# Crossbar turns of q', k' and x for pairs 5 to 11 in a gated recurrence followed by a GELU layer, with the whole order of the work written out

## The chip, the cores and the metric

The kernel runs on one core of one Trainium2 chip. The metric is the device time of one execution in microseconds; before the change the median of three runs is 177.12 us (177.09 to 177.12). Profiles and traces come from one further execution, recorded by the hardware profiler; its times start at the first instruction.

## What is computed

```
# q, k, v, alpha: (4, 8, 768, 48) f32; w_in: (384, 2048); w_out: (2048, 384)
for t in range(768):
    state = alpha[:, :, t, :, None] * state + k[:, :, t] (x) v[:, :, t]     # outer product, 48 x 48 a head
    y[:, :, t] = q[:, :, t] @ state
x = y with the 8 heads of a token side by side                              # (3072, 384)
out = gelu_tanh(x @ w_in) @ w_out                                           # (3072, 384) f32
```

Four sequences, eight heads of 48 features, 768 time steps; each head carries a 48 by 48 state that decays by alpha per feature. The result feeds two dense layers.

## The kernel before

**Chunks and pairs.** Time is cut into 6 chunks of 128 tokens. A *pair* is one chunk of two sequences; there are 12, m = 0 to 11, pair m being chunk m // 2 of sequences 2(m % 2) and the next. A *unit* is one sequence of a pair. Within a chunk the recurrence becomes matrix products:

- `ln` (ScalarE, L361): the logarithm of alpha; `cum` (TensorE, L378): its running sum over the tokens, by a product with a triangle of ones. In all but the last chunk `cum` also makes, with L380, the sums over the whole chunk, feature by feature, in eight products of one column a pair.
- `b`, `binv` (ScalarE, L407): the exponentials of plus and minus the running sum, in bf16; `bend` (L401): that of the whole chunk's sum, which `end` (VectorE, L516) spreads into the two halves of 64 features.
- `qp`, `kp` (VectorE, L418): q' = q b and k' = k binv, each head padded to 64 features.
- the turn of q' and k' so that features lie on partitions. For pairs 0 to 6 TensorE does it: `t` (L428) are transposes into PSUM, `ev` (L446) the eviction into `qkT`. For pairs 7 to 11 (`TURN_QK`) the crossbar does it: `turn` m.0 (q') and m.1 (k'), transposing DMAs issued by the SP queue (L466).
- `attn` (TensorE, L489): 16 products on half arrays of 64 rows, giving the scores of both units; `mask` (VectorE, L496) keeps the causal half.
- `y` (TensorE): four products of 96 columns with the carried state (L543) and eight of 48 columns with v (L546) for each unit; `x` copies the result into bf16 (L553).
- the turn of x: for pairs 0 to 5 on TensorE (`tx`, L560, and `xe`, L564), for pairs 6 to 11 (`TURN_X`) by one DMA for each unit (L472).
- `kv` (TensorE, L506) and `st` (VectorE, L528 and L531): the state for the next chunk.
- `l1` (TensorE, L572): first dense layer of the pair, 8 tasks of 6 products; `gelu` (ScalarE, L578) after each; `l2` (TensorE, L591): second layer, 4 tasks of 4 products a unit; `ot` (copy out of PSUM, L603) and `store` (SP queue, L616). Pairs 0 and 1 share one second layer, named `l20`.

A task is named by kind, pair and number: `attn5.0` is the score task of pair 5, `l15.0` the first task of its first layer, `store2.0` a store of pair 2's first unit.

**Loads.** 66 loads. The first 12 are issued by SP and ScalarE; the rest by POOL, in the order of `LOADS`, with two gates near the start only (`gatea 0 1`, `gatek 0 1`): a small POOL copy that waits for an early load, so that later ones do not overtake it. A load of a, q, k or v of a pair takes 384 KB from HBM; v is narrowed to bf16 on the way. Each kind has five or six buffers (`BUFS`), and a load waits until its buffer's last reader is done.

**Order.** `Scheduler.order` decides the order in which every engine gets its tasks, on paper, before the program is built. Up to some 46 us the order is written out by hand in `FIRST` ("P:attn0.0" is TensorE, V VectorE, A ScalarE, G POOL, S the SP queue). After that a list scheduler takes over with the costs in `W` and `COST`; `late_qk` and `late_x` are allowances by which it takes a crossbar turn of an early pair to land later. Each engine then works off its own list strictly in order, and waits where an operand or a buffer isn't ready. The SP queue issues turns and stores in one list. `DECAYS` groups the logarithms and exponentials of pairs between two runs of gelus, since ScalarE must load a table whenever it changes between them.

Of the kernel before, what the change touches and what calls it, by code (L numbers as in the profile page):

```python
# [16 lines left out]
    cum=530, cum_packed=1500, t8=450, t4=225, attn=340, kv=170, inter=170, intra=205, tx=168, l1_4=655, l1_2=340, l2=655,  # L17
    qk2=910, qk1=500, ev8=650, ev4=350, mask=640, st=1090, st0=545, end=110, attn2=590, vb=320, vb_act=480, ring=1300, ring_issue=670, out=2050, lead=600, receipt=1400, receipt_hw=1000, xc=520, xe=330, ot=540,
    ev8_act=960, ev4_act=520, xc_act=450, xe_act=450, ot_act=450,
    strip=1700, cast=1900, weight=2080, dma=2100, issue=1100, wissue=760, sp=100, store=2600, turn=1250, landed=2200, xbar_qk=1500, xbar_x=1000, late_x=2500, late_qk=1200, piece=330, late_k=1500, piece_issue=450, begin=620, cast_0=1300, share=1200, cast_1=1900, ln_packed=1040, cold=380, fill=216, zero=1100,  # L20
# [26 lines left out]
class Scheduler:  # L47
# [16 lines left out]
    def order(self):  # L64
# [5 lines left out]
        def given(tag):  # L70

            n, at = len(taken[tag]) - self.bufs[tag], 0
            for u in taken[tag][n] if n >= 0 else ():
                if u.done is None:
                    return None
                at = max(at, u.done)
            return at

        def ready(t, inorder=True):
# [7 lines left out]
            for tag, _ in t.takes:  # L87
                g = given(tag)
                if g is None:
                    return None  # L90
                at = max(at, g)
# [80 lines left out]
class _Kernel:  # L172

    BLOCKS = ((0,), (1,), (2,), (3,), (4,), (5,), (6,), (7,), (8,), (9,), (10,), (11,))
    DECAYS = {-1: (0, 1), 1: (2, 3), 2: (4,), 3: (5,), 4: (6, 7), 5: (8,), 6: (9,), 7: (10,), 8: (11,)}

# [10 lines left out]
        A:table.0 A:load.2 A:load.3 S:load.0 S:load.1 S:load.4 A:ln0.0 S:load.5 P:fill.7 P:cum0.0 A:ln0.1 G:gate.0 G:load.12 S:load.6 P:cum0.1 A:b0.0 S:load.7  # L187
        A:bend0.0 V:qp0.0 A:binv0.0 A:binv0.1 S:load.8 V:kp0.0 P:fill.2 P:t0.0 A:b0.1 V:ev0.0 P:fill.1 P:t0.1 S:load.9 A:ev0.1 V:qp0.1 S:load.10 A:bend0.1
        P:fill.3 P:attn0.0 V:kp0.1 G:gate.1 S:load.11 P:t0.2 G:load.13 V:mask0.0 A:ev0.2 P:t0.3 G:load.14 V:mask0.1 A:ev0.3 P:fill.1 P:t0.4 V:ev0.4 P:fill.1
        P:attn0.1 A:ln1.0 G:load.15 P:t0.5 V:mask0.3 P:cum1.0 A:ev0.5 G:load.16 V:vb0.0 A:ln1.1 V:end0.0 P:y0.0 V:mask0.2 G:load.17 P:kv0.0 A:binv1.0 P:cum1.1  # L190
        V:st0.0 A:x0.0 G:load.18 A:vb0.1 V:kp1.0 P:tx0.0 A:b1.0 P:y0.1 V:xe0.0 G:load.19 V:qp1.0 P:t1.1 A:x0.1 A:bend1.0 G:load.20 A:b1.1 P:fill.1 P:t1.0
        A:ev1.0 V:ev1.1 G:load.21 V:qp1.1 P:fill.1 P:kv0.1 V:st0.1 G:load.22 A:binv1.1 P:tx0.1 P:attn1.0 V:xe0.1 G:load.23 P:t1.2 V:kp1.1 P:l10.0 A:ev1.2
        G:load.24 V:mask1.0 P:t1.3 A:bend1.1 P:t1.4 V:mask1.1 G:load.25 A:ev1.3 P:l10.1 V:ev1.4 G:load.26 A:vb1.0 P:t1.5 P:attn1.1 G:load.27 V:ev1.5 P:y1.0
        G:load.28 P:l10.3 V:end1.0 V:vb1.1 V:mask1.2 G:load.29 A:gelu0.0 P:kv1.0 P:l10.2 V:mask1.3 A:x1.0 G:load.30 P:l10.5 A:gelu0.1 V:st1.0 A:gelu0.3 P:y1.1
        G:load.31 P:l10.4 A:gelu0.5 V:x1.1 P:tx1.0 A:gelu0.2 P:tx1.1 P:l10.6 G:load.32 V:xe1.1 A:gelu0.4 V:xe1.0 P:l10.7 A:gelu0.6 G:load.33 P:l11.0 A:gelu0.7
        P:l11.6 A:gelu1.0 P:l11.5 A:gelu1.6 P:l11.7 A:gelu1.5 P:l11.2 A:gelu1.7 P:l11.4 A:gelu1.2 P:l11.3 A:gelu1.4 P:l11.1 A:gelu1.3 P:kv1.1 P:l20.0
        A:gelu1.1 P:l20.4 P:l20.1 A:ln2.0 P:l20.2 P:cum2.0 P:l20.5 A:b2.0 A:binv2.0 P:l20.9 A:bend2.0 V:kp2.0 A:ln2.1 P:l20.6 V:st1.1 P:cum2.1 V:qp2.0 P:l20.8
        A:b2.1 A:binv2.1 P:t2.0 P:l20.3 V:kp2.1 A:ev2.0 V:qp2.1 P:l20.10 A:bend2.1 P:attn2.0 P:t2.1 V:mask2.1 P:l20.7 A:ev2.1 V:mask2.0 P:l20.14 A:ln3.0
        P:attn2.1 P:y2.0 V:mask2.2 P:l20.13 V:mask2.3 P:l20.12 V:x2.0 P:cum3.0 A:ot0.0 V:ot0.1 P:y2.1 A:ot0.2 S:store0.0 S:store0.1 P:tx2.0 P:l20.11 A:x2.1
        S:store0.2 V:xe2.0 A:b3.0 P:tx2.1 P:l20.15 V:xe2.1 A:binv3.0 V:end2.0 P:l12.0 V:ot0.3 A:bend3.0 P:l12.1 V:qp3.0 S:store0.3 P:kv2.0 P:l12.2 V:st2.0  # L200
        A:gelu2.0 P:l12.3 V:end3.0 V:kp3.0 A:gelu2.1 P:l12.4 A:gelu2.2 P:t3.0 A:gelu2.3 P:t3.1 A:gelu2.4 V:ev3.0 P:l12.5
# [9 lines left out]
    TURN_QK, TURN_X = (7, 8, 9, 10, 11), (6, 7, 8, 9, 10, 11)  # L211
# [10 lines left out]
    BUFS = dict(ca=1, yk=2, ff=4, la=3, qp=4, kp=4, b8=2, kn=2, qkT=4, atm=6, x=3, ot=5, bend=3, ends=8,  # L222
                a=6, q=5, k=5, vb=6)

    def __init__(self, ctx, tc, q, k, v, alpha, w_in, w_out, out):
# [22 lines left out]
        self.ones = const.tile([C, 1], F16, name="ones")  # L248
# [3 lines left out]
        self.half = const.tile([C, 2], F32, name="half")  # L252
        self.state = [[const.tile([C, H // 2, 2 * D], BF16, name=f"st{b}_{i}") for i in range(2)]
                      for b in range(B)]
        self.ring = {n: [const.tile([C, 2, H, 64], F16 if n == "la" else BF16, name=f"{n}{i}")
                         for i in range(self.BUFS[n])] for n in ("la", "qp", "kp")}
# [54 lines left out]
    def wait(self, r, m, j):  # L311

        u = self.p[list(self.p)[m]]
        return lambda e: self.nc.gpsimd.tensor_copy(self.gate[:, 0:1], u[r][:, j, 0, 0:1])
# [606 lines left out]
```

## Time and profile before

| | |
|---|---|
| median of three runs | 177.12 us |
| span of the profiled execution, first to last instruction | 175.3 us |
| what lies around the span, against the median | 1.8 us |
| first product of l10.0, TensorE | 16.91 us |
| last product of the second layer ends, TensorE | 172.66 us |
| POOL's last load issued | 88.28 us |
| first crossbar turn issued (x of pair 6) | 93.11 us |
| median from issue to landing: turn of q' or k' | 2.8 us |
| median from issue to landing: turn of x, one unit | 2.3 us |
| median from issue to landing: loads of a, q, k, v by POOL | 11.6 to 12.5 us |
| TensorE clock granted | 1.00 throughout |

How to read the profile: the page gives each engine's busy time, then the span in 40 equal slices (4.4 us each) whose digits are tenths busy, then DMA queues, then the chain of work that ended last. q0 is the queue of POOL's loads, q1 that of the transfers issued by SP; a DMA's packets are spread over 16 DMA engines, and shares of a short stretch can exceed 100% because packets of the two queues overlap on an engine. A product's duration includes its way through the array, so a run of products is priced by the distance between starts. "PE" is TensorE, "PEld" its weight loads, "DVE" VectorE, "ACT" ScalarE, "POOL" GpSimd, "SPq" the SP queue.

### The profile page before, as it was taken

The numbers are of one execution on the slowest core, as the hardware profiler recorded it, in microseconds if no ns is written. First come the engines' busy times: TensorE is split into PE (matmuls) and PEld (weight loads), VectorE is DVE, ScalarE is ACT, GpSimd is POOL, SyncE is SP. The second block draws the span as 40 slices with busy tenths as digits, with TensorE's granted clock in tenths as the row PEclk, the third lists the DMA queues.
The fourth block names the chain that finished last, engine by engine and source line by source line (L and its number), as shares of the span: only waits on it lengthen the run. The fifth ranks groups of instructions, "written<-read, shape, count | busy, mean of one in ns | idle before, by whom it ended". The sixth has DMA issues, their size and how long they took to land.

```text
span 175.3 us, 4440 instructions
## 1 busy us (share of the span) xinstructions
PE 170.4 (97%) x1845; PEld 135.4 (77%) x1845; DVE 96.8 (55%) x192; ACT 128.9 (74%) x213; POOL 57.7 (33%) x64
## 2 busy tenths in 40 slices
PE   7989999999999999999999999999999999999993
PEld 2667999667987896797798698698697697796973
DVE  6499920356888993795598897495426405000000
ACT  4677999666968668768788967977987984481941
POOL 2496348977645776576720000000000000000000
PEclk9999999999999999999999999999999999999999
DMA  4999999999999999999999992271271360401102
GB/s 138 307 262 224 210 243 238 246 205 207 249 273 204 242 256 220 217 226 199 200 264 224 200 136 80 54 172 52 47 187 28 90 165 4 115 20 49 45 0 90
DMA packets 49620, 28.86 MB, mean 165 GB/s; under 512 B 37696, under 2 KB 46016, under 8 KB 49600
## 3 DMA queue, kind: packets, MB, share of 16 engines
q0 software_dynamic: 26464, 17.70, 60.8%
q1 hardware_dynamic: 22592, 10.49, 24.8%
q10 hardware_dynamic: 544, 0.39, 0.8%
q8 instruction: 14, 0.23, 0.6%
q14 instruction: 6, 0.05, 0.1%
HBM read 25.17 MB, written 4.72 MB: 170 GB/s over the span
## 4 chain that ended last, share of the span: by engine, by line
PE 90%; DMA 6%; DVE 1%; issue 0%; ACT 0%; SPq 0%; POOL 0%
PE hT L572 36%; PE acc L591 36%; DMA v<-in_v_dram 4%; PE at L489 4%; PE qkT_ps L428 3%; PE yps L546 3%; PE kv L506 2%; PE yps L543 2%; DMA a<-in_alpha_dram 2%; PE cum L378 2%; PE xT_ps L560 1%; PE cum L380 1%; SPq L305 0%; ACT qkT L446 0%; DVE vb L389 0%
## 5 line engine op out<-in xcount | busy, mean ns | idle before, releaser
L572 PE MATMUL hT<-xT,w_in 128*128 128x256 bf16 x576 | 69.4, 273 | 0.0
L578 ACT ACTIVATE gT<-hT 128x512 bf16<-128x512 f32 x96 | 56.3, 600 | 17.7 <-PE hT L572 14.2
L591 PE MATMUL acc<-w_out,gT 128*128 128x384 bf16 (+3 forms) x416 | 69.0, 313 | 0.0
L572 PEld LDWEIGHTS <-w_in 128*128 128x128 bf16 x576 | 61.1, 114 | 1.6
L591 PEld LDWEIGHTS <-gT 128*128 128x128 bf16 x416 | 36.9, 98 | 19.2
L496 DVE TENSOR_TENSOR atm<-at,ut 128x512 bf16<-128x512 f32 x48 | 30.1, 681 | 12.7 <-PE at L489 12.6
L418 DVE TENSOR_TENSOR qp<-q,b 128x768 bf16<-128x768 f32 (+1 forms) x15 | 11.9, 794 | 14.0 <-ACT b L407 11.7
L418 DVE TENSOR_TENSOR kp<-k,binv 128x768 bf16<-128x768 f32 (+1 forms) x15 | 11.9, 791 | 10.6 <-ACT binv L407 10.6
L603 ACT COPY ot<-acc 128x384 f32<-128x384 f32 (+3 forms) x17 | 7.4, 439 | 13.0 <-PE acc L591 12.9
L308 POOL DMA_DIRECT2D k<-in_k_dram x11 | 12.2, 1107 | 6.6 <-DVE atm L496 3.0
L308 POOL DMA_DIRECT2D vb<-in_v_dram x11 | 12.1, 1102 | 6.7 <-PE hT L572 1.7
L308 POOL DMA_DIRECT2D q<-in_q_dram x11 | 12.2, 1109 | 6.1 <-DVE atm L496 1.3
L308 POOL DMA_DIRECT2D a<-in_alpha_dram x11 | 12.2, 1114 | 5.9 <-DMA w_in<-in_moe_w_in_dram 1.3
L407 ACT ACTIVATE b<-cum 128x768 bf16<-128x768 f32 (+1 forms) x15 | 10.3, 683 | 3.6 <-PE cum L380 2.3
L280 ACT ACT_TABLE_LOAD x9 | 11.5, 1283 | 0.9 <-PEq L905 0.7
L578 ACT ACT_TABLE_LOAD x9 | 11.5, 1283 | 0.2
L407 ACT ACTIVATE binv<-cum 128x768 bf16<-128x768 f32 (+1 forms) x15 | 10.2, 681 | 0.1
L528 DVE TENSOR_TENSOR stmp<-kv,st 128x384 f32<-128x384 f32 x16 | 8.8, 552 | 2.0 <-PE kv L506 2.0
L553 DVE CAST x<-yps 128x384 bf16<-128x384 f32 x12 | 6.7, 556 | 4.7 <-PE yps L546 4.7
L531 DVE TENSOR_TENSOR st<-stmp,ends 128x384 bf16<-128x384 f32 x16 | 8.9, 558 | 0.6
L446 ACT COPY qkT<-qkT_ps 128x512 bf16<-128x512 bf16 (+1 forms) x9 | 6.5, 728 | 3.7 <-PE qkT_ps L428 3.5
L546 PE MATMUL yps<-vb,atm 128*128 128x48 bf16 x192 | 8.7, 183 | 0.4 <-DVE vb L389 0.4
(65 smaller groups left out, 156.7 us busy)
## 6 DMA issues: line engine op xcount, KB each, us to landing
out_dram<-ot SPq DMA_DIRECT2D x19, 192.0 KB, 5.2
a<-in_alpha_dram POOLq DMA_DIRECT2D x9, 384.0 KB, 12.5
q<-in_q_dram POOLq DMA_DIRECT2D x9, 384.0 KB, 11.6
k<-in_k_dram POOLq DMA_DIRECT2D x9, 384.0 KB, 11.7
vb<-in_v_dram POOLq DMA_DIRECT2D x9, 192.0 KB, 11.6
w_in<-in_moe_w_in_dram POOLq DMA_DIRECT2D x4, 384.0 KB, 9.3
w_out<-in_moe_w_out_dram POOLq DMA_DIRECT2D x4, 384.0 KB, 11.1
out_dram<-ot SPq DMA_DIRECT2D x9, 96.0 KB, 1.8
```

What stands on the lines that cost most here:

```text
L280: nc.scalar.add_instruction(mybir.InstLoadActFuncSet(name=nc.get_next_instruction_name(), act_func_set_id=i, engine=mybir.EngineType.Activ ...
L308: dma(u[t][:, lo:hi].rearrange("t b h d -> t (b h) d"), src.rearrange("b h s d -> s (b h) d")[c * C:(c + 1) * C])
L407: self.nc.scalar.activation(u[n].rearrange("t i h d -> t i (h d)")[:, lo:hi], cum, AF.Exp, scale=1.0 if n == "b" else -1.0)
L418: self.nc.vector.tensor_tensor(out, rows, b, op=ALU.mult)
L496: self.nc.vector.tensor_tensor(u["atm", i][:, o], u["at", i][o], self.ut[:, None, :].to_broadcast([self.C, self.H // 2, self.C]), op=ALU.mult)
L528: nc.vector.tensor_tensor(s, acc, old, op=ALU.add)
L531: nc.vector.tensor_tensor(new.rearrange("f p (o d) -> f (p o) d", o=2), acc.rearrange("f p (o d) -> f (p o) d", o=2), ends, op=ALU.mult)
L546: nc.tensor.matmul(y[:, h, :], u["atm", i][:, h % 2, h // 2, :], u["vb"][:, i, h, :], start=c == 0, stop=True, skip_group_check=True)
L572: self.nc.tensor.matmul(h[:, s], w_in[:, j, nt % 4 + s], self.xT[c % self.NX][:, j, lo:hi].rearrange("p g t -> p (g t)"), start=j == 0, st ...
L578: return lambda e: self.nc.scalar.activation(self.gT[c % self.NG][:, nt:nt + 2, lo * self.C:hi * self.C], f.pop(("h", c, lo, nt)), AF.Gelu ...
L591: self.nc.tensor.matmul(f["acc", c, b][:, lo:hi], self.gT[c % self.NG][:, nt, b * self.C:(b + 1) * self.C], self.w_out[:, nt, lo:hi], star ...
L603: self.copy(e)(f["ot", c, b][:, sl], f["acc", c, b] if half is None else f["acc", c, b, half][:, sl])
```

## The change

- The crossbar turns q' and k' of pairs 5 to 11 (before 7 to 11) and x of pairs 5 to 11 (before 6 to 11), and x as one DMA for both units of a pair; the layout of `xT` becomes unit by unit.
- The chunk's end decay is no longer a product and an exponential: from pair 2 on, four small VectorE transposes (`tr`) of 32 by 32 blocks take the last row of `b`, which is now kept in f32 in a padded ring; `end` reads from that. L380 and, from pair 2 on, `bend` are gone.
- For pairs 3 to 11 (`INTER`) the product with the carried state becomes part of the task `attn`: 16 products of 64 rows and 48 columns into two PSUM tiles, one for each half of the heads; `y` adds the eight products of its half of the heads for both units.
- `FIRST` now holds the whole order to the end, tasks of the two layers of neighbouring pairs interleaved; `DECAYS` is gone.
- `LOADS` is unchanged; all loads are issued in the order of their numbers. `wait` and `held` learn to wait for a turned tile, and no entry of `LOADS` uses that.
- The last pair's second unit is now done before its first; the program ends with `ot11.0` and `store11.0`, a whole 128 by 384 tile.

```diff
@@ the order, the part around the first two crossbar pairs (A ScalarE, P TensorE, V VectorE, S the SP queue)
+        P:cum4.0 A:b4.0 A:binv4.0 V:mask3.1 P:y3.0 P:l22.5 P:l22.6 V:x3.0 V:qp4.0 P:y3.1 A:x3.1 P:l22.3 P:cum5.0 V:kp4.0 P:tx3.1 P:tx3.0 V:xe3.1
+        A:ot2.0 P:l22.7 V:xe3.0 P:t4.1 V:tr4.0 A:binv5.0 V:kp5.0 P:t4.0 P:l13.0 A:b5.0 V:ev4.1 S:store0.0 V:tr4.1 V:tr4.2 V:tr4.3 V:ev4.0 V:end4.0
+        A:ot2.1 S:turn5.1 S:store2.0 P:l13.7 A:gelu3.0 A:gelu3.7 P:kv4.1 P:l13.2 P:l13.5 P:l13.6 P:kv4.0 A:gelu3.2 S:store0.1 V:st4.1 A:gelu3.6
+        A:gelu3.5 P:l13.1 P:l13.4 A:gelu3.1 P:l13.3 A:gelu3.4 V:st4.0 V:qp5.0 V:tr5.0 P:attn4.0 V:mask4.2 S:turn5.0 V:mask4.0 V:mask4.1 V:mask4.3
+        P:l23.4 A:gelu3.3 P:l23.5 P:l23.6 P:y4.0 P:l23.7 V:tr5.1 V:ot3.1 V:tr5.2 A:ln6.0 P:y4.1 P:cum6.0 P:l23.0 A:x4.0 V:tr5.3 V:end5.0 A:x4.1
+        P:tx4.1 V:xe4.1 S:store3.1 S:store0.3 A:binv6.0 P:tx4.0 V:xe4.0 P:l23.1 V:kp6.0 P:kv5.0 P:l23.2 A:b6.0 A:ln7.0 V:st5.0 P:l14.0 P:kv5.1 P:l23.3
+        P:l14.7 A:gelu4.0 A:ot3.0 A:gelu4.7 P:l14.1 A:gelu4.1 V:st5.1 G:load.47 G:load.48 G:load.49 P:attn5.0 G:load.50 G:load.51 V:tr6.0 S:turn6.1
+        S:store2.1 P:l14.6 P:l14.4 V:qp6.0 V:mask5.0 V:mask5.1 S:turn6.0 A:gelu4.6 P:l14.3 P:l14.5 A:gelu4.4 A:gelu4.3 A:gelu4.5 P:l14.2 V:tr6.1
+        V:mask5.2 V:mask5.3 P:y5.0 P:y5.1 P:l24.4 V:x5.0 V:x5.1 V:tr6.2 P:cum7.0 P:kv6.1 A:gelu4.2 P:l24.0 P:l24.1 P:kv6.0 V:tr6.3 V:end6.0 V:st6.1
+        A:b7.0 P:l24.5 P:l24.6 V:qp7.0 A:binv7.0 V:st6.0 A:ln8.0 P:cum8.0 A:b8.0 A:binv8.0 P:l24.7 P:l24.2 P:l24.3 P:attn6.0 A:ot4.1 S:turn5.2 V:tr7.0
...
+        P:l211.6 P:l211.7 P:l211.8 P:l211.9 V:ot10.0 S:store10.0 P:l211.0 S:store10.1 V:ot11.1 A:ot11.2 V:ot11.3 S:store11.1 S:store11.2 S:store11.3
+        P:l211.1 P:l211.2 P:l211.3 A:ot11.0 S:store11.0
...
-    TURN_QK, TURN_X = (7, 8, 9, 10, 11), (6, 7, 8, 9, 10, 11)
+    TURN_QK, TURN_X = (5, 6, 7, 8, 9, 10, 11), (5, 6, 7, 8, 9, 10, 11)
+    INTER = (3, 4, 5, 6, 7, 8, 9, 10, 11)
...
-        self.xT = [const.tile([C, self.NKT, B, C], BF16, name=f"xT{c}") for c in range(self.NX)]
+        self.xT = [const.tile([C, B, self.NKT, C], BF16, name=f"xT{c}") for c in range(self.NX)]
...
-                for p in range(H // 2) if u["sums"] else ():
-                    nc.tensor.matmul(cum[:, i, H * D + p:H * D + p + 1],
-                                     la[:, i, 2 * p:2 * p + 2, :].rearrange("t h d -> t (h d)"),
-                                     self.ones, start=True, stop=True, skip_group_check=True)
...
-    def turn_x_dma(self, u, i, c, b):
-        return lambda e: self.nc.sync.dma_start_transpose(self.xT[c % self.NX][:, :, b, :], u["x", i])
+    def turn_x_dma(self, u, c, b):
+        return lambda e: self.nc.sync.dma_start_transpose(
+            self.xT[c % self.NX][:, b:b + 2].rearrange("d u j t -> d (u j) t"), u["x"].rearrange("t u n -> t (u n)"))
...
+            if carried:
+                c, b = carried
+                y = [self.tile("yk", [C, 2, H // 2, self.D], F32, "yps") for _ in range(2)]
+                for i in units:
+                    st = self.state[b + i][c % 2]
+                    for p in range(H // 2):
+                        for o in range(2):
+                            sl = slice(64 * o, 64 * o + 64)
+                            nc.tensor.matmul(y[o][:, i, p, :], u["T"][sl, 0, i, p, :], st[sl, p, self.D * o:self.D * o + self.D],
+                                             start=(i, p) == (0, 0), stop=False, skip_group_check=True)
...
+    def last_row(self, u, o, half):
+        C, H, D = self.C, self.H, self.D
+        def emit(e):
+            if "tr" not in u:
+                u["tr"] = self.tile("kn", [C, H, 64], F32, "tr")
+            rows = u["rows"][96:128]
+            lo, f = o * D + 32 * half, 64 * o + 32 * half
+            self.nc.vector.transpose(u["tr"][f:f + 32, :, 0:32], rows[:, lo:lo + H * 2 * D].rearrange("t (g n) -> t g n", n=2 * D)[:, :, 0:32])
+        return emit
...
+    def y_heads(self, u, o):
+        def emit(e):
+            y = u["y", o]
+            for i in range(2):
+                for p in range(self.H // 2):
+                    self.nc.tensor.matmul(y[:, i, p, :], u["atm", i][:, o, p, :], u["vb"][:, i, 2 * p + o, :],
+                                          start=False, stop=True, skip_group_check=True)
+        return emit
...
-        s = self.s = Scheduler(self.BUFS, self.fill, 60000, self.FIRST, self.LANDED)
+        s = self.s = Scheduler(self.BUFS, self.fill, 0, self.FIRST, self.LANDED)
```

## The prediction

> **What bounds the kernel now.** I read the page's busy shares first, then the 40 slices, the waits of TensorE, the chain, and last the DMA view by stretches.
>
> ```profile
> span 175.3 us, 4440 instructions
> ...
> PE 170.4 (97%) x1845; PEld 135.4 (77%) x1845; DVE 96.8 (55%) x192; ACT 128.9 (74%) x213; POOL 57.7 (33%) x64
> ...
> PE   7989999999999999999999999999999999999993
> ...
> DMA  4999999999999999999999992271271360401102
> ...
> PE 90%; DMA 6%; DVE 1%; issue 0%; ACT 0%; SPq 0%; POOL 0%
> ```
>
> TensorE is busy in every slice from the fourth to the last but one, the chain is TensorE for 90%, and asked for TensorE's waits between 20 us and the end, the trace names none. From 17 us on the time is the sum of TensorE's instructions, and what keeps that so is that every operand lies ready before its product's turn comes. The second long row of nines is the DMA's: full until the 24th slice, about 100 us, because the 66 loads run without a break (the last is issued at 88.28 us and lands some 11 us later). Until 93 us this kernel puts no transpose on the DMA engines. The change does.
>
> A few rows tell what a transfer of the SP queue meets there. First the stretch 94 to 95 us, loads still running, with one turn of x started at 93.11 (packets, MB, share; then us to landing):
>
> ```profile
> q0 software_dynamic: 302, 0.19, 115.9%
> q1 hardware_dynamic: 82, 0.02, 10.7%
> ...
> xT<-x SPq DMA_TRANSPOSE x1, 5.9
> ```
>
> Then 99 to 100 us, loads over, turns alone:
>
> ```profile
> q1 hardware_dynamic: 1173, 0.28, 128.4%
> ```
>
> q0 carries POOL's loads, q1 what SP issues. In a microsecond beside loads q1 gets 82 packets through, alone 1173: a fourteenth. Over 94.2 to 96 us it is 133 packets, 8.3 for each of 16 engines in 1.8 us, **0.22 us a packet and engine**; alone it is 0.014. Stores of 192 KB (144 packets, 9 an engine) say the same of the time between 40 and 90 us: 143 packets of q1 in 62 to 65.5 us are 0.39 us each, 288 in 73 to 78 us are 0.28; they land after 5.2 to 8.9 us, against 1.9 once the loads are over. I take 0.3, with 0.22 and 0.39 as ends.
>
> **What the change takes from TensorE.** All prices are distances between starts in the timeline.
> - The column sums (L380): four products from 69.34 to the next start at 69.45, 27 ns each, 8 a pair, 8 pairs: 64 x 0.027 = 1.7 us gone.
> - q' and k' of pairs 5 and 6: 16 transposes from 59.01 to the next start at 59.90, 0.89 us a pair: 1.8 us gone. x of pair 5: two times 0.17, 0.34 us gone.
> - The product with the carried state, pairs 3 to 11: before, two times four products of 96 columns, 0.17 us each, 0.34 a pair. After, 16 products on half arrays, 48 columns each. No row shows it. Ends: one weight load after another at L380's 27 ns, 16 x 0.027 = 0.43; or two halves side by side, as the sixteen half-array products of L489 need 0.555 against the eight's 0.33, that is 0.028 each for 128 columns, so by columns 0.17. I take 0.22, nearest to L489, which is the same form on the same tile: 0.12 x 9 = 1.1 us gone (ends: 1.5 gone, 0.8 added).
>
> [...] No run here has the 48-column form yet.
>
> Sum: 4.9 us less. TensorE's last product ends at 172.66 us now and would end at 167.8.
>
> **What is moved off the path and costs nothing there.** Four small transposes a pair on VectorE (bounds: 0.16 us as the 16-element row of L516, 0.55 as a 384-element f32 row; I take 0.3, 32 of them 9.6 us) against 2.8 us of evictions of pairs 5 and 6 and 0.7 of pair 5's x: 6 us more on an engine that is 55% busy; at 0.55 a pair costs 2.2 us, still within VectorE's idle time (28 of 62 us between 92 and 154). ScalarE loses the bend exponentials and two of 18 table loads (1.28 us each). The f32 decays enter products that already read one f32 operand. x as one turn of six blocks instead of two turns of three saves an issue of 1.2 us on SP. All of it is hidden by a TensorE that waits for none of it; should VectorE fall behind, masks come late, which belongs to the rivals.
>
> **Tail.** The last unit now ends with one 384-column copy (0.476 against 0.212) and one 192 KB store (1.9 against 1.5): 0.7 us more after the last product, 3.3 instead of 2.6.
>
> **What is added: a wait.** That no load waits for a turn changes nothing by itself: the list of loads and its two gates are the same in both kernels, and the new code that could hold a load for a turn is not used. TensorE takes its list in order, and attn5.0 now waits for the crossbar. Summing the new list with the prices above from l10.0 at 16.9 us, and shifting by the 0.8 us that such a sum lacks against the trace by then, attn5.0's turn comes at **74 us**. On SP stand, in order, store0.0, turn5.1 (k'), store2.0, store0.1, turn5.0 (q'). kp5.0 is ready at 58.3, qp5.0 at 64.3 by the same sum. A turn of q' or k' is eight blocks: between 139 and 143.8 us two of them account for 2176 small packets, so 1088 each, 68 an engine. From 58.3: issue 1.3, the store ahead 2.7, k' 68 x 0.3 = 20, two stores 5.4, q' 20 again: 108 us. That lies past the end of the loads, and there the price falls to 0.014. So the end of the loads decides. They drain at about 97 us now (in 96 to 99 us q0 has only 17% left); the new order issues them back to back and no buffer holds them (all but the last v, which needs y5, find their buffers free before attn5.0), and the turns' own packets add some 150 x 0.02 = 3 us an engine. Loads over at about 100; q' lands at 99 to 101.5. With 0.22 us a packet it lands at 96. I take 99.5: **TensorE stands for 25.5 us** at attn5.0. Behind it wait l14.6 and everything after, on ScalarE the gelus, on VectorE mask5; POOL doesn't wait. k', q' of pair 6 and x of pair 5 queue behind, but by then the queue is quick and attn6.0 is 11 us further on: no second stall of size.
>
> [...]
>
> After so long an idle time TensorE may start slow: the first seven idle products of the program take 3.26 us, where 512 columns at the later pace (256 in 0.109) would make 1.53. I add 1.6 us, between nothing and 1.7.
>
> Sum against the profiled execution: 167.8 + 25.5 + 1.6 + 3.3 = 198.2 us of span. The median of the runs, 177.12, is 1.8 above the span of 175.3, so **200.0 us**. With q' landing between 92 and 104, and the product of pairs 3 to 11 at its ends: 191 to 207.
>
> **Rivals.**
> - *The turns keep up* (faster). Place: attn5.0. It decides at the pace: 154 packets an engine (k', two stores, q') in the 14.4 us from 59.6 to 74 allow 0.094 us a packet. If transposed packets go through at that or better, no stall is left beyond some tenths, and the time is 177.1 - 4.9 + 0.7 + 0.3 = 173.2. For it: turns alone need 0.014, and the planner's own allowance is only 1.2 us more for pairs under 8. Against: every stretch with loads shows over twice 0.094. Chance 0.15.
> - *Half a stall*: loads with many 96-byte packets (v) let turns through at about half my price. Then 154 x 0.15 + 61 gives 84 us, a stall of 10, and pair 6's turns and x5, due at 84 and 85 on the old clock, add a few: 184 to 190. Chance 0.12.
> - *The product on half arrays costs 0.43 and small waits appear* (the x turns of pairs 8 and 9 have 4.3 to 4.8 us from y to the layer that reads them, against 0.8 for the copy and 2.6 for the turn) without a long stall: 175 to 178. Chance 0.03.
> - The forecast: 0.70.
>
> Slower, then, in 0.82; within 0.2% (0.35 us, about what runs of this kernel can tell from no change) 0.02; faster 0.16. The range takes in the forecast's and most of the half stall: 182 to 208.
>
> **What would show it.** In the profile after: one idle stretch of TensorE between about 74 and 99 us, put down to the DMA of qkT, with the chain's DMA share up by some 13%; turns of qp and kp of pair 5 landing after 20 to 40 us; q1 under 150 packets a microsecond between 60 and 95. TensorE's busy sum would be 4 to 6 us lower. If turns of pair 5 land within 9 us, the forecast is wrong and 173 is right; if the loads end long before or after 100, the stall moves with them.

## The result and the profile after

| | before | after |
|---|---|---|
| median of the runs | 177.12 us (177.09 to 178.23) | 203.14 us (200.88 to 209.36) |
| span of the profiled execution | 175.3 us | 202.0 us |
| TensorE busy | 170.4 us | 172.4 us |
| mean granted TensorE clock | 1.00 | 0.94 |
| POOL's last load issued | 88.28 us | 113.47 us |
| landing of a turn, q' / k' / x (median; x of one unit before, of a pair after) | 2.8 / 2.8 / 2.3 us | 5.4 / 10.4 / 3.4 us |

The changed kernel takes 1.141 times as long (95% interval 1.134 to 1.149). Ratios, here and below, leave out runs over 1.5% above the fastest of the same kernel as slow; where a trace is of such a run (e3, e4, e5, e7, e8), its section says so. From the page of the changed kernel: the span, the busy shares, three rows of the 40 slices (5.05 us each), the queues and the chain by engine.

```profile
span 202.0 us, 4381 instructions
PE 172.4 (85%) x1813; PEld 134.0 (66%) x1815; DVE 110.5 (55%) x223; ACT 122.5 (61%) x200; POOL 57.7 (29%) x64
PE   7989999989999990897024957999999999999993
PEclk9999999999999998599855897999999999999999
DMA  5999999999999999999999999973312607305031
PE 63%; DMA 27%; DVE 5%; ACT 3%; issue 1%; ACTq 0%
```

TensorE's row of nines has holes between slices 16 and 25, some 75 to 125 us, and the clock row dips to 5 behind them. The DMA row stays full through slice 26, to about 131 us, where before it was full through slice 24, to about 105. The last load lands at 113.47 + 18.2 = 131.7 us; before it was 88.28 + 10.3 = 98.6. The chain has 27% of DMA in place of 6%. The waits of TensorE from 20 us on name the transfers (us in total, times, longest):

```profile
PE at L524 <- DMA qkT<-qp: 15.7, 2, 9.6
PE at L524 <- DMA qkT<-kp: 3.8, 1, 3.8
PE hT L647 <- DMA xT<-x: 3.5, 1, 3.5
```

23.0 us in four pieces. The timeline shows where, with the idle time ahead of each in brackets:

```profile
81.71 1.04 PE L524 MATMUL at<-qkT 64*128 64x128 bf16 x16 [6.12 <-DMA qkT<-qp]
104.02 1.04 PE L524 MATMUL at<-qkT 64*128 64x128 bf16 x16 [9.58 <-DMA qkT<-qp]
108.89 6.11 PE L647 MATMUL hT<-xT,w_in 128*128 128x256 bf16 x36 [3.52 <-DMA xT<-x]
122.66 0.62 PE L524 MATMUL at<-qkT 64*128 64x128 bf16 x16 [3.81 <-DMA qkT<-kp]
```

These are attn5.0, attn6.0, l15.0 and attn7.0: the scores of pairs 5 to 7 and the first layer of pair 5, all fed by the crossbar while loads run. On the SP queue the same stretch reads (start, time that the issue took):

```profile
60.32 2.65 SPq L500 DMA_TRANSPOSE qkT<-kp  x1
66.38 2.26 SPq L500 DMA_TRANSPOSE qkT<-qp  x1
74.00 8.86 SPq L500 DMA_TRANSPOSE qkT<-kp  x1
83.83 7.45 SPq L500 DMA_TRANSPOSE qkT<-qp  x1
91.36 6.77 SPq L506 DMA_TRANSPOSE xT<-x  x1
```

Before, an issue took 1.2 to 1.5 us. Here those of pair 6 took 7 to 9 us and each of the two turns landed 20.1 us after it began; k' and q' of pair 5 landed after 10.4 and 15.2. POOL suffers as well: three times it stands still for 10 to 11 us, each time released by a load of v that lands late (the one issued at 66.43 us landed 30.2 us later, and POOL went on at 96.91).

```profile
81.38 1.15 POOL L345 DMA_DIRECT2D k<-in_k_dram  x1 [11.20 <-DMA vb<-in_v_dram]
96.91 1.15 POOL L345 DMA_DIRECT2D k<-in_k_dram  x1 [10.09 <-DMA vb<-in_v_dram]
112.20 1.15 POOL L345 DMA_DIRECT2D k<-in_k_dram  x1 [10.10 <-DMA vb<-in_v_dram]
```

So turns and loads seem to slow each other: the last load is issued 25 us later than before, and that gives later turns more loads to meet. The experiments test this.

### The profile page after: what moved, and what is told of

It reads as the page before. It is cut to its first block, busy times and chain, and to the rows that moved or that the text cites. A ratio compares the mean times of both kernels' runs of the same rounds, so it can differ in the third digit from the quotient of the medians.

```text
span 202.0 us, 4381 instructions
## 1 busy us (share of the span) xinstructions
PE 172.4 (85%) x1813; PEld 134.0 (66%) x1815; DVE 110.5 (55%) x223; ACT 122.5 (61%) x200; POOL 57.7 (29%) x64
## 3 DMA queue, kind: packets, MB, share of 16 engines
q0 software_dynamic: 26464, 17.70, 59.1%
## 4 chain that ended last, share of the span: by engine, by line
PE 63%; DMA 27%; DVE 5%; ACT 3%; issue 1%; ACTq 0%
PE hT L647 26%; PE acc L666 23%; DMA qkT<-qp 17%; DMA qkT<-kp 9%; PE at L524 3%; PE idle L326 2%; PE qkT_ps L462 2%; DVE atm L543 2%; DVE tr L567 2%; PE cum L383 1%; PE yps L616 1%; PE kv L553 1%; ACT qkT L480 1%; ACT gT L653 1%; PE cum L415 1%
## 5 line engine op out<-in xcount | busy, mean ns | idle before, releaser
L653 ACT ACTIVATE gT<-hT 128x512 bf16<-128x512 f32 x96 | 53.6, 602 | 39.4 <-PE hT L647 37.3
L647 PE MATMUL hT<-xT,w_in 128*128 128x256 bf16 x576 | 72.3, 281 | 4.0 <-DMA xT<-x 3.5
L666 PE MATMUL acc<-w_out,gT 128*128 128x384 bf16 (+3 forms) x416 | 70.6, 318 | 0.0
L647 PEld LDWEIGHTS <-w_in 128*128 128x128 bf16 x576 | 62.4, 115 | 7.6 <-DMA xT<-x 3.7
L524 PE MATMUL at<-qkT 64*128 64x128 bf16 x192 | 8.8, 233 | 19.7 <-DMA qkT<-qp 15.7
L524 PEld LDWEIGHTS <-qkT 64*128 64x128 bf16 x192 | 6.2, 101 | 23.8 <-issue 17.4
L678 ACT COPY ot<-acc 128x384 f32<-128x384 f32 (+1 forms) x16 | 7.5, 469 | 16.5 <-PE acc L666 16.3
L678 DVE COPY ot<-acc 128x384 f32<-128x384 f32 (+2 forms) x10 | 5.0, 504 | 20.4 <-PE acc L666 20.3
L441 ACT ACTIVATE binv<-cum 128x768 bf16<-128x768 f32 (+1 forms) x15 | 10.3, 684 | 8.2 <-PE cum L415 7.8
L567 DVE STREAM_TRANSPOSE tr<-b 32x256 f32<-32x256 f32 x32 | 14.0, 438 | 1.1 <-ACT b L441 0.4
L345 POOL DMA_DIRECT2D a<-in_alpha_dram x11 | 12.3, 1115 | 6.2 <-ACT la L398 2.1
L441 ACT ACTIVATE b<-cum 128x768 f32<-128x768 f32 (+1 forms) x15 | 10.3, 685 | 3.9 <-PE cum L415 2.1
## 6 DMA issues: line engine op xcount, KB each, us to landing
vb<-in_v_dram POOLq DMA_DIRECT2D x9, 192.0 KB, 18.2
```

The source lines that it names most:

```text
L345: dma(u[t][:, lo:hi].rearrange("t b h d -> t (b h) d"), src.rearrange("b h s d -> s (b h) d")[c * C:(c + 1) * C])
L441: self.nc.scalar.activation(u[n].rearrange("t i h d -> t i (h d)")[:, lo:hi], cum, AF.Exp, scale=1.0 if n == "b" else -1.0)
L524: nc.tensor.matmul(at[o][:, p, :], t[sl, 1, p, :], t[sl, 0, p, :], start=True, stop=True)
L567: self.nc.vector.transpose(u["tr"][f:f + 32, :, 0:32], rows[:, lo:lo + H * 2 * D].rearrange("t (g n) -> t g n", n=2 * D)[:, :, 0:32])
L647: self.nc.tensor.matmul(h[:, s].rearrange("p (g t) -> p g t", t=self.C), w_in[:, j, nt % 4 + s], self.xT[c % self.NX][:, lo:hi, j], start= ...
L653: return lambda e: self.nc.scalar.activation(self.gT[c % self.NG][:, nt:nt + 2, lo * self.C:hi * self.C], f.pop(("h", c, lo, nt)), AF.Gelu ...
```

## The experiments

**Theory A**: a crossbar turn that meets loads crawls, whatever is loaded; TensorE waits for it, and the end of the loads decides when that stops. **Rivals**: the new order or the other new parts (the state product, the last-row transposes) cost the time; the kind of load (v in 96-byte pieces) decides; the loss of each turn is local, without an effect on what comes later. Times are medians of runs of the same kernel; the kernel before ran beside each at 177.15 to 177.24 us.

### e1: the loads taken away

```diff
+    KEEP = 6
+            if u["m"] >= self.KEEP:
+                u[t] = list(self.p.values())[self.KEEP - 1][t]
+                return
```

> The changed kernel, its order and its turns as they are, but POOL loads nothing for pairs 6 to 11: their a, q, k and v are read from pair 5's tiles (left out: 24 of the 66 loads, so the output of the later chunks is not the reference's). The loads are then over at about 57 us, before the first turn of pair 5 at 60 us. Theory (turns are slow beside POOL's loads, and TensorE waits for them in order): every turn lands 2.6 to 3.5 us after its issue, attn5, l15.0, attn6 and attn7 wait for nothing, and the time is 173 to 175 us. Rival (the written-out order itself, or the new turns as such, hold TensorE up): the stalls of 6.1, 9.6, 3.5 and 3.8 us remain and the time stays above 195.

Measured 174.87 us (174.73 to 175.01), ratio 0.987 [0.985, 0.989]. Two lines of its page and its two waits from 20 us on:

```profile
span 172.9 us, 4326 instructions
PE 165.9 (96%) x1813; PEld 130.5 (75%) x1815; DVE 109.9 (64%) x223; ACT 122.5 (71%) x200; POOL 30.1 (17%) x40
...
PE hT L651 <- DVE xT L643: 0.5, 1, 0.5
PE kv L557 <- DVE xT L643: 0.2, 1, 0.2
```

With the same order and the same instructions on TensorE, no wait for a DMA is left, and the clock stays at 1.00. The rival "order" falls, and with it the thought that the stores ahead of the turns in SP's list cost the time: that list is the same here. The time is 1.7 us above the forecast's no-stall case of 173.2, which comes back below. This run also gives the sum: TensorE idles 172.9 - 165.9 = 7.0 us here and 202.0 - 172.4 = 29.6 us in the changed kernel, so **22.6 us are idle time**, and its products take 172.4 - 165.9 = **6.5 us** longer. 22.6 + 6.5 is the whole difference of 29.1 us. The lower clock accounts for the 6.5: in stretches of 5 us from 75 to 130 us, busy time times the missing share of the clock makes 6.0 us.

### e2: the turns alone

On the kernel before:

```diff
-    TURN_QK, TURN_X = (7, 8, 9, 10, 11), (6, 7, 8, 9, 10, 11)
+    TURN_QK, TURN_X = (5, 6, 7, 8, 9, 10, 11), (5, 6, 7, 8, 9, 10, 11)
```

> The kernel before with one edit: the crossbar turns q' and k' of pairs 5 and 6 and x of pair 5 as well; order, sums and state product as before (the planner places the new turns itself). Theory (turns beside loads): the turns of pairs 5 to 7 land after 10 to 20 us, TensorE waits for them for 20 to 30 us in sum, and the time is 195 to 208. Rival (the written-out order is what stalls): 174 to 178, since 2.1 us of transposes leave TensorE.

Measured 202.92 us (202.22 to 204.41), ratio 1.147 [1.141, 1.153]. The waits:

```profile
PE at L489 <- DMA qkT<-kp: 14.6, 3, 7.5
PE hT L572 <- DMA xT<-x: 7.0, 1, 7.0
```

The two tuples alone lose as much as the whole change does, 25.8 against 26.0 us: 21.6 us of waits and a clock of 0.941, with the old planner, the old end decay and the old state product.

### e3: pairs 5 and 6 back on TensorE

On the changed kernel, its order edited for the tasks that come back:

```diff
-    TURN_QK, TURN_X = (5, 6, 7, 8, 9, 10, 11), (5, 6, 7, 8, 9, 10, 11)
+    TURN_QK, TURN_X = (7, 8, 9, 10, 11), (6, 7, 8, 9, 10, 11)
```

> The changed kernel with q' and k' of pairs 5 and 6 and x of pair 5 turned by TensorE again (4 transposing tasks, 2 for x, with their evictions on VectorE put into the order); everything else as changed. Theory: no turn before pair 7 meets the loads, so the stalls at attn5, l15.0 and attn6 go; the turns of pair 7, issued at about 88 us while loads run to some 97, still cost 2 to 4 us at attn7. 177.1 less 2.8 (sums, state product), plus 0.7 (tail), plus 1 (the small transposes of pairs 2 and 3 on the path), plus 3: 178 to 180, or 175 to 176 without the stall at attn7. Rival (order): 195 or more.

Measured 190.49 us (183.6 to 191.16). The expectation of 178 to 180 was missed by 3.6 us in the fastest run and by 10 to 11 in the other three. In the trace, which is of a run of 190.14 us, one wait is large:

```profile
PE at L528 <- DMA qkT<-kp: 8.3, 1, 8.3
```

The loads are as early as before (the last is issued at 88.08 us), but the new order issues pair 7's turns at 87.03 and 91.62 us, and the issue of the second took 6.14 us. The two landed after 16.6 and 16.1 us. In the kernel before, the first turn of q' starts at 95.08 us and lands after 4.8. What makes a turn safe is not its pair but that it starts when the loads drain; how long this wait is in the run of 183.6 us isn't shown.

### e4: loads held back for the turns

On the changed kernel, gates that hold the loads of pairs 8, 9, 10 and 11 until turns of pairs 5, 6, 7 and 8 have landed:

```diff
-    LOADS = (..., '6', '7', '8', '9', '10', '11')
+    LOADS = (..., '6', '7', 'gateT 5 0', '8', 'gateT 6 0', '9', 'gateT 7 1', '10', 'gateT 8 0', '11')
```

> The changed kernel with four gates in POOL's list: the loads of pair 8 wait until q' of pair 5 is turned, those of pair 9 for q' of pair 6, of pair 10 for k' of pair 7, of pair 11 for q' of pair 8. Nothing else changes. Theory: a turn then meets at most the four to seven loads already on their way; the turns of pair 5 land some 8 to 12 us after issue, those of 6 and 7 within 5 to 8, the stalls shrink from 23 us to 3 to 10, and the time is 177 to 186. If the loads that are held come too late for pairs 8 to 11, a wait for them takes the stall's place and the time stays at 185 to 195. Rival (SP's list of stores and turns is the bottleneck, whatever POOL does): 200.

Measured 187.24 us (185.72 to 190.02), ratio 1.054 [1.048, 1.060]: 16 us better than the change, and 1 us past the upper end that I gave the theory. In the trace, of a run of 190.02 us, waits of TensorE for turns fall from 23.0 to 10.1 us:

```profile
PE at L528 <- DMA qkT<-qp: 5.2, 1, 5.2
PE hT L651 <- DMA xT<-x: 4.9, 3, 2.1
```

attn5.0 waits for nothing now. But a gate lets a turn of the pair ahead through, and the next pair's turns then meet the loads that it released; POOL stood for 14.9, 12.5, 1.2 and 14.0 us at the four gates, and the last load went out at 122.33 us.

### e5: two turns that nobody reads

On the kernel before, with q' and k' of pair 5 turned a second time into spare tiles:

```diff
+        self.spare = [const.tile([C, 2, H // 2, C], BF16, name=f"spare{i}") for i in range(2)]
...
+            if u["m"] == 5:
+                self.nc.sync.dma_start_transpose(self.spare["qk".index(n)].rearrange("d i p t -> d (i p) t"),
+                                                 u[n + "p"].rearrange("t i h d -> t (i h d)"))
```

> The kernel before, with two crossbar turns added that nobody waits for: as soon as q' and k' of pair 5 are made (about 72 us), SP also turns them into two spare tiles; TensorE still turns them for the computation. Theory (a turn beside loads is slow by itself, whoever reads it): the two land 10 to 20 us after their issue, against 2.8 alone, and POOL's pace of 1.7 us a load stretches while they are under way; TensorE waits for nothing before 93 us; the loads end some 4 to 6 us later, so that x of pair 6 and q', k' of pair 7 meet them and cost 0 to 6 us: 177 to 183. Rival (the turns were late because stores or an unfinished operand stood before them in SP's list): they land within 5 us and the time is 177.

Measured in two runs 190.38 and 193.39 us, median 191.89, far over the 177 to 183 expected; the trace is of the second. The spare turns, issued at 71.62 and 73.22 us, landed after 8.8 and 12.3 us. POOL stopped behind them, its last load went out at 94.48 us in place of 88.28, and then the kernel's own turns, which used to start as the loads drained, met them:

```profile
84.55 1.15 POOL L309 DMA_DIRECT2D a<-in_alpha_dram  x1 [5.55 <-ACT b L408]
...
113.72 1.47 PE L576 MATMUL hT<-xT,w_in 128*128 128x256 bf16 x6 [12.85 <-DMA xT<-x]
```

The first line names b on ScalarE as what released the load, but the run without spare turns has no such stop, and e12 has it at the same place. The second line is 40 us after the spare turns: the price is paid by x of pair 6. "The loss is local" falls, if the reading is right; e12 was made to test it.

### e6: no loads of v from pair 6 on

```diff
+            if n == "v" and u["m"] >= 6:
+                u[t] = list(self.p.values())[5][t]
+                return
```

> The changed kernel without the v loads of pairs 6 to 11 (left out: v of these pairs is read from pair 5's tile, the output of the later chunks is not the reference's). It asks which loads the turns suffer from, those of a, q and k (packets of some 4 KB) or those of v (2048 packets of 96 bytes a load). Theory A (any load; an engine serves one large packet for each small one of a turn, 0.2 to 0.3 us a packet and engine): with a, q and k alone the turns are slower by the packet than in the changed kernel, attn5 comes later than 81.7, at about 87 to 92 when the 18 loads are over, then nothing waits: 188 to 195. Theory B (the 96-byte packets are what the turns and the loads block each other with): without them turns of pair 5 land within 8 us, POOL's three pauses of 10 us vanish and the time is 175 to 182.

Measured 191.99 us (191.87 to 192.12), ratio 1.083 [1.079, 1.086]. One stall is left:

```profile
90.94 1.03 PE L527 MATMUL at<-qkT 64*128 64x128 bf16 x16 [15.48 <-DMA qkT<-qp]
```

q' of pair 5, issued at 66.24 us, landed after 24.6 us (15.2 with the loads of v); the last load was issued at 78.28 us, and by 91 us it is over. This is the single stall that the prediction described, with an earlier end of loads. Loads of a, q and k alone are enough, so "v decides" falls as the cause. Loads of v do have a part of their own: without them POOL's stops of 10 us are gone, and the first turns crawl longer. The packets of the two queues show how (q0 the loads, q1 turns and stores; packets, MB, share), here from 70 to 80 us, then in the changed kernel from 95 to 100 us:

```profile
q0 software_dynamic: 559, 1.96, 93.6%
q1 hardware_dynamic: 565, 0.14, 10.5%
...
q1 hardware_dynamic: 837, 0.24, 97.5%
q0 software_dynamic: 827, 0.27, 70.0%
```

In both stretches nearly one packet of the loads goes through for each packet of q1; so it does in some stretches of 2 us of the changed kernel (505 to 505 in 96 to 98 us, 160 to 160 in 108 to 110), but not in all (604 to 422 in 100 to 102). Without v a load's packet has 3.5 KB, and a turn's packet costs 10 us x 16 / 565 = 0.28 us an engine. A load of v has 2064 packets (q0 carries 26464 in the changed kernel and 14080 here, six loads fewer), one of a, q or k 112. With these among the loads a packet of q0 has 0.33 KB in the second stretch and a turn's costs 0.10 us, but all queues together move only 104 GB/s, and the loads fall behind. Packet size isn't the whole of it: over stretches of 2 us from 74 to 110 us the changed kernel's price runs from 0.06 to 0.34 us.

### e7 and e8: the rest of the change with the turns of before

The kernel before with the state product of the change and x as one turn a pair (e7), and with the last-row transposes from pair 4 on as well (e8). Against the changed kernel, beside the order and the planner of before:

```diff
-    TURN_QK, TURN_X = (5, 6, 7, 8, 9, 10, 11), (5, 6, 7, 8, 9, 10, 11)
+    TURN_QK, TURN_X = (7, 8, 9, 10, 11), (6, 7, 8, 9, 10, 11)
+    LAST = 99
```

LAST is the first pair whose end decay comes from the last row: 99 in e7, 4 in e8.

> The parts of the change that leave the crossbar alone, first half: turns, order and planner as before, but the product with the carried state of pairs 3 to 11 goes onto half arrays inside the score task, and x of a pair is turned by one DMA. The changed kernel's trace has the 16 products at 0.20 us against 0.34 before: 9 times 0.14, so 1.2 us less, 175.9. Rival: both state tiles now occupy the two small PSUM buffers from the scores to the copies, which delays the products for the next state, and the time is 177 or more.

> As the one before, and from pair 4 on the end decay comes from the last row by four small transposes on VectorE instead of eight products and an exponential. 6 pairs at 0.21 us of TensorE: another 1.3 us less, 174.6. Rival: the transposes (0.44 us each in the changed kernel's trace, 1.8 us a pair) put the masks behind and TensorE waits for them: 176 or more. If turns of pair 7 now start 2 us earlier, beside the last loads, a wait at attn7 of some us would show as well.

Measured: e7 197.95 us (194.27 to 199.33), ratio 1.103 [1.096, 1.109]; e8 206.97 us (200.06 to 209.67). Even the fastest runs lie 18 and 25 us above what was expected; the traces are of runs of 198.75 and 204.85 us. A stall of e7, then two of e8:

```profile
119.27 1.04 PE L498 MATMUL at<-qkT 64*128 64x128 bf16 x16 [18.07 <-DMA qkT<-kp]
```

```profile
115.37 1.03 PE L498 MATMUL at<-qkT 64*128 64x128 bf16 x16 [11.07 <-DMA qkT<-kp]
...
127.79 2.50 PE L621 MATMUL hT<-xT,w_in 128*128 128x256 bf16 x11 [11.06 <-DMA xT<-x]
```

The tuples are those of before, and pair 7's q' is issued only 2 (e7) and 4 us (e8) earlier than there; the loads came 7 to 8 us late. POOL issued one each 2.0 to 2.1 us from 55 us on, against 1.75 before, and the last at 96.14 (e7) and 95.64 us (e8). Pair 7's turns, issued at 93.10 and 94.62 us in e7, met them, and the issue of the second took 11.23 us. Between 45 and 90 us the DMA engines moved 209 GB/s in e7 against 232 before. Why is not settled: before 90 us no turn had been issued.

### e9 and e10: turns later still

e8 with the turns moved back by one and by two pairs (e9, then e10):

```diff
-    TURN_QK, TURN_X = (7, 8, 9, 10, 11), (6, 7, 8, 9, 10, 11)
+    TURN_QK, TURN_X = (8, 9, 10, 11), (7, 8, 9, 10, 11)
```

```diff
-    TURN_QK, TURN_X = (7, 8, 9, 10, 11), (6, 7, 8, 9, 10, 11)
+    TURN_QK, TURN_X = (9, 10, 11), (8, 9, 10, 11)
```

> The kernel before with the change's state product and its last-row transposes (as in the run named e8_best), but the crossbar turns q' and k' only from pair 8 and x only from pair 7. TensorE has 0.89 us of transposes of pair 7 and 0.34 us of x of pair 6 back, so without a stall 174.6 + 1.2 = 175.8 us. Theory (turns must not meet loads): in the kernel before pair 8's turns are issued at 100.2 and 101.6 us and the loads are over at some 97 to 100. If POOL issues its last load by 90 us, no stall of TensorE over 1 us and 175 to 177. If the loads are as slow as in e7 and e8 (2.0 us a load, the last issued at 96), these turns still meet them and the time is 185 to 200. Rival (the state product or the last row cost time by themselves, without the turns): 190 or more with the turns landing in 3 us.

> As e9, but q' and k' turned only from pair 9 and x from pair 8, so that no turn is issued before some 110 us. Without a stall 174.6 + 2 x 0.89 + 2 x 0.34 = 177.1 us, the same as the kernel before. Theory (turns must not meet loads): 176 to 178 whatever the pace of the loads, all turns landing in 2 to 4 us, no wait of TensorE for a DMA over 1 us after 20 us. Rival (the new parts or their slower loads cost time by themselves): 185 or more.

Measured: e9 186.69 us (186.18 to 186.95), ratio 1.053 [1.050, 1.055]; e10 186.63 us (186.34 to 188.03), ratio 1.054 [1.050, 1.058]. The stalls of e8 are gone, and 13 us with them against its fastest run: in e9 TensorE waits for no turn, in e10 for 1.0 us in two pieces. But 10.9 and 9.5 us more than the 175.8 and 177.1 without a stall remain, and for e10 it is the rival's number that came. Another engine holds TensorE up. The stretches of e9 (from and to, length in us, then busy time of PE, PEld, DVE, ACT, POOL, the clock, the DMA share, GB/s):

```profile
90.00:95.00 5.00, 5.00 (x54) 4.72 (x52) 4.79 (x9) 4.52 (x9) 2.96 (x3) 1.00 1.23 221
95.00:100.00 5.00, 5.00 (x44) 3.31 (x42) 4.70 (x11) 3.59 (x5) 1.15 (x1) 1.00 1.51 179
100.00:105.00 5.00, 2.69 (x57) 1.72 (x55) 4.96 (x9) 1.22 (x3) 0.00 (x0) 1.00 1.44 194
105.00:110.00 5.00, 3.00 (x19) 2.06 (x20) 4.02 (x10) 1.85 (x3) 0.00 (x0) 0.68 1.22 146
110.00:115.00 5.00, 4.97 (x57) 3.97 (x55) 2.48 (x4) 2.04 (x4) 0.00 (x0) 0.64 0.27 46
```

VectorE (DVE) is busy 18.5 of the 20 us from 90 to 110, and TensorE idles 4.3 us there, put down mostly to masks (atm) and evictions on VectorE; then its clock is 0.64 to 0.68 for 10 us, which on 8.0 us of busy time is another 2.7. Four last-row transposes of 0.44 us a pair and the evictions of the pairs given back to TensorE are on VectorE's list; that they are what it lacked time for was not tested apart. In e10 the same 20 us hold 3.2 us of idle time, and a clock of 0.66 from 105 to 110 costs 1.4. Some 4 us of each run I can't place.

### e11 and e12: the two spare turns again, with later turns

e11 is the kernel before with the tuples of e10; e12 is e11 with the spare turns of e5.

```diff
-    TURN_QK, TURN_X = (7, 8, 9, 10, 11), (6, 7, 8, 9, 10, 11)
+    TURN_QK, TURN_X = (9, 10, 11), (8, 9, 10, 11)
```

> The kernel before with q' and k' turned by the crossbar only from pair 9 and x from pair 8; nothing else differs. TensorE gets two pairs of q' and k' and two of x back: 177.1 + 1.8 + 0.7 = 179.6 us under every theory (179 to 180.5). It is the partner of e12.

> e11 with the two extra turns of pair 5's q' and k' into spare tiles that nobody reads, as in the run named e5_probe, which cost 14.7 us there. Theory (the extra turns cost nothing themselves; they delay the loads by some 6 us, and only turns that then meet the loads cost time): the same as e11 within 1 us, with POOL's last load issued 4 to 8 us later than in e11. Rival (late loads themselves, or the extra turns' traffic, hold TensorE up): 5 us or more above e11.

Measured: e11 183.01 us (182.39 to 184.67), ratio 1.033 [1.027, 1.040]; e12 182.09 us (181.52 to 182.75), ratio 1.027 [1.024, 1.030]. e11 was expected at 179 to 180.5: attn9.0 waits 2.1 us for a k' that the planner issues late, and its clock is 0.91 over 120 to 140 us. The comparison is what counts. The landings of e12's spare turns, its last load and its one wait:

```profile
spare<-qp SPq DMA_TRANSPOSE x1, 8.6
spare<-kp SPq DMA_TRANSPOSE x1, 13.7
```

```profile
84.82 1.15 POOL L309 DMA_DIRECT2D a<-in_alpha_dram  x1 [6.01 <-ACT b L408]
...
93.30 1.15 POOL L309 DMA_DIRECT2D k<-in_k_dram  x1 [0.50 <-DVE x L557]
```

```profile
PE at L493 <- DMA qkT<-kp: 1.9, 1, 1.9
```

The same two turns delay the loads as in e5 (last issue 93.30 us against 88.01 in e11), and now they cost nothing: 0.9 us less than e11, where e5 lost 13.1 us in its faster run and 14.7 in the median. Each probe differs from its partner by the same two turns; between the two partners only the tuples differ, and with them whether later turns meet the late loads (the first turn that is read is issued at 93.02 us in e5, at 113.96 in e12). That settles how the loss travels: **turns delay loads, and the late loads catch the next turns.**

## Why the prediction was right

The forecast was 200.0 us, the time is 203.14, and the bound named (attn5.0 behind turns beside loads, the end of the loads deciding) is in part what the runs show: e1 and e2 bear out that turns beside loads are the cause, but the end of the loads moved to 132 us, and the stall at attn5.0 ended at 81.7, long before it. By its steps:

- **TensorE's savings, 4.9 us: right.** e1 against before has 170.4 - 165.9 = 4.5 us less busy time. The state product, valued at 0.22 us between 0.17 and 0.43, takes 0.20 us in the chain.
- **The cover on VectorE: sized low, and thinner than I said.** A last-row transpose takes 0.44 us, not 0.3; 32 take 14.0 us. In e1 the span is 172.9 us where the forecast without a stall gives 167.8 + 3.3 = 171.1, and the chain of e1 has 12% of VectorE; l12.0 starts 0.6 us later than before. In the order of e9 TensorE idles 4.3 us where VectorE is nearly full. ScalarE keeps all of its 18 table loads; the prediction took two away.
- **Tail, 3.3 us: right.** The last product ends at 198.6 us, 3.4 before the end.
- **attn5.0 due at 74 us: right.** It is due at 81.71 - 6.12 = 75.6 us.
- **One stall of 25.5 us at attn5.0 and "no second stall of size": wrong in shape, near in sum.** 6.1, 9.6, 3.5 and 3.8 us make 23.0. Two steps of it failed. First the price: pair 5's turns landed after 10.4 and 15.2 us, which for 68 packets an engine is 0.15 and 0.22 us, not 0.3. That is the premise of the rival *half a stall*, loads of v letting turns through, and e6 bears it out: without v q' needed 24.6 us, 0.36 a packet, and 0.28 in the stretch shown there. In e6's stretch 559 packets of the loads went through beside 565 of q1, in the changed kernel's 827 beside 837; in the prediction's own row it is 302 beside 82. Second, "the turns' own packets add some 150 x 0.02 = 3 us an engine" to the loads, and "POOL doesn't wait": POOL stood still three times, 31.4 us in all, its last load went out 25 us later, so the loads were over not at 100 but at some 132 us, and the turns of pairs 6 and 7 and of pair 5's x met them. The first error took 19 us off the first stall, the second put 17 us of new stalls behind it. That they nearly cancel is luck, and so the time is right while its course isn't.
- **Slow start after the stall, 1.6 us: too small.** Slower products cost 6.5 us (e1). There were four stalls, not one, and the granted clock of the stretches 80 to 85 and 100 to 110 us is 0.50, as the last three lines below show.

Stretches of the changed kernel, columns as above:

```profile
75.00:80.00 5.00, 0.59 (x6) 0.33 (x3) 1.61 (x3) 1.17 (x2) 0.00 (x0) 0.89 1.55 160
80.00:85.00 5.00, 3.29 (x42) 2.71 (x43) 2.61 (x5) 0.49 (x1) 3.21 (x3) 0.50 1.58 145
100.00:105.00 5.00, 0.98 (x23) 0.98 (x24) 0.36 (x1) 0.00 (x0) 2.03 (x2) 0.50 1.70 106
105.00:110.00 5.00, 1.48 (x24) 1.03 (x19) 2.74 (x6) 0.00 (x0) 0.00 (x0) 0.50 1.40 196
```

The last column but one says that the DMA engines are as occupied as before (1.40 to 1.70, against 1.04 to 1.93 in the stretches between 60 and 90 us of the kernel before; such a share exceeds 1 even with one queue alone, 1.28 in the row of 99 to 100 us), and the last that less is moved: 106 to 196 GB/s, against 196 to 263.

By stretches of 1 us the changed kernel's clock is 1.00 from 73 to 78 us, 0.50 from 79 to 85, 1.00 from 86 to 99, 0.50 from 100 to 113, 1.00 from 114 to 123, 0.50 from 124 to 126 and 1.00 from 127 to 135; the six stretches in between have 0.64 to 0.99. The mean of 0.70 from 110 to 115 us is 0.50 up to 113 and 0.99 to 1.00 behind it. The clock falls while TensorE stands (the stalls that end at 81.71 and 104.02 us) or just after (the one that ends at 122.66); in e1, without a stall, it is 1.00 over the whole run. No run shows more of its cause.

Turns beside loads alone cost e2 25.8 us. The kernel before issues its first turn at 93.11 us, with the last load issued at 88.28 and landed at 98.6: turns only as the loads drain, by a margin of a few microseconds.

Against the signs that the prediction named: TensorE's busy time fell by 4.5 us only in e1, and in the changed kernel the clock hides it; the chain's DMA share rose by 21 points, not 13; q1 moved 226 packets a microsecond in 66 to 70 us, above the 150 named, and 71 to 158 in the 5 us stretches from there to 90 us; the landings of 20 us came with pair 6, not 5.

It stays open why e7 to e10 load at 2.0 us a piece, and why a load of k waits on POOL for one of v to land. e3, with the same state product but the change's order, has its last load at 88.08 us, so the state product alone is no answer. Several orders of the turns that the gates of e4 suggest, with all turns of a pair let through before its loads, weren't tried.

## What to carry to other kernels

Price a transposing DMA by what else the DMA engines carry when it runs (here a turn of q' or k' landed after 2.8 us, the median before, and after 10.4 to 20.1 us in pairs 5 and 6 of the changed kernel), and then price what it does to those transfers (here the last load went out 25 us later): a transfer that nobody waits for can still be the one that makes a later wait. When a kernel's first crossbar turns sit just behind its last loads, the distance between the two is a margin to be measured ahead of any change that shifts either, for 6 us of delay cost 13 us or more here (e5). And work moved to an engine that is 55% busy on average, as VectorE was, may land in a stretch where that engine is 92% busy, as in e9.

## What the runs showed of the hardware that was not expected

- A turn stops POOL's loads, not only the reverse: stops of 5.6 to 6.0 us behind two turns (e5, e12), 10 to 11 us in the changed kernel; loads of v landed after 18.2 us (median) in place of 11.6. Without v loads (e6) the stops of 10 us are gone.
- The issue on SP itself takes up to 8.9 us in the changed kernel and 11.2 us in e7, against 1.2 to 1.5 alone, so stores behind it in the list wait too.
- Executions of one kernel can lie far apart when its turns meet loads: 200.9 to 209.4 us for the changed kernel and 200.1 to 209.7 for e8, against 177.1 to 178.2 before and 174.73 to 175.01 in e1. They needn't: e2 has 202.2 to 204.4 us.
- In some stretches with turns and loads under way, the two queues moved nearly the same number of packets, those of the loads first: 559 to 565 in 10 us of e6, 827 to 837 in 5 us of the changed kernel, 505 to 505 in 2 us of it (96 to 98).
- The granted clock was 0.50 from 79 to 85, 100 to 113 and 124 to 126 us, during the stalls and after them: the slower products make 6.5 us on top of the 23.0.
